# Attention and channel mix on one core: the weights' last bits on ScalarE, the last keys transposed as 64 columns, and a new early order

## The chip, the cores and the metric

The kernel runs on one core of one Trainium2 chip. The metric is the device time of one execution in microseconds (us); the kernel before takes 636.65 us as the median of three runs (635.62 to 637.12). The core has five engines with a queue each: TensorE (PE; its weight loads are listed as PEld), VectorE (DVE), ScalarE (ACT), GpSimd (POOL) and SyncE (SP), which here issues nearly all the DMAs.

## The reference, cut to what matters

There are 8 batches of 576 tokens, 8 heads of 64, a model width of 512 and a hidden width of 1024. Keys and values are averaged over groups of 8 tokens, so each batch has 72 of them. The attention's output is the input of a channel mix with a shift by one token.

```python
def _attn_ref(q, k, v):
    k_p = k.reshape(B, H, Sp, pool, D).mean(axis=3)
    v_p = v.reshape(B, H, Sp, pool, D).mean(axis=3)
    scores = scale * np.matmul(q, k_p.transpose(0, 1, 3, 2))
    scores = scores - np.max(scores, axis=-1, keepdims=True)
    attn = np.exp(scores)
    attn = attn / (np.sum(attn, axis=-1, keepdims=True) + 1e-09)
    return np.matmul(attn, v_p).astype(np.float32)

def _moe_ref(x, mu_k, mu_r, w_k, w_v, w_r):
    x_prev = np.concatenate([np.zeros((B, 1, D)), x[:, :-1, :]], axis=1)
    xk = mu_k * x + (1.0 - mu_k) * x_prev
    xr = mu_r * x + (1.0 - mu_r) * x_prev
    k = np.maximum(xk @ w_k, 0.0)
    v = k * k @ w_v
    r = 1.0 / (1.0 + np.exp(-(xr @ w_r)))
    return (r * v).astype(np.float32)
```

The three weight matrices are float64 in memory; everything else is float32.

## The kernel before, in words

**Tiles, chunks, precision.** The 4608 tokens are cut into 36 tiles of 128 rows and 12 chunks of 3 tiles (384 tokens). Matrix products of full precision are done in one of two ways. In chunk 0 the operands are float32 as they are ("whole"), which costs PE two passes for each product. From chunk 1 on each operand is split into a rounded high part and a low part (type fp32r), and a product is three: high by high, low by high, high by low.

**Weights.** They arrive as 20 blocks of 128 x 512 float64 words: wk0 to wk7 for the hidden layer, wr0 to wr3 for the gate, wv0 to wv7 for the output. `convert` (L415) turns the two 32-bit words of each number into a float32 by integer arithmetic, in five steps: ACT takes the absolute value of the top word (L427); DVE takes the maximum with a tiny number (L429), shifts left by 3 and masks (L431), merges sign and exponent (L436), and merges the low word's last three bits (L441). Later `split` (L450) makes a block's high part on ACT (L463) and its low part on DVE or POOL (L466, chosen by `LOW_BY`). There is one block of memory more than there are weight blocks, so the splits go one after another.

**Attention.** `keys`, `values` and `last_values` sum the eight tokens of each group: on DVE or POOL by halving (L473), or on PE as products with the identity (L484, "t" in `SUM_BY`). `softmax` (L572) does one tile: scores on PE (L592), then maximum, subtraction, exponential, sum and division, on DVE and ACT; for the tiles in `BY_HEAD` ACT does the eight heads one by one with the sum included (L614). The division is on POOL or DVE (`NORM_BY`). The 72 columns of a head are handled as 64 plus 8 ("last keys"), since PE takes 128 rows at a time: the 64 of two heads fill one transpose. `transposed` (L656) transposes the 64-column parts, four transposes a tile (L667). `transposed_rest` (L686) does the last keys: DVE copies the 8 columns of the eight heads twice in rounded form and once as the rest (L698, L700), so that there are 2 x 96 columns; PE transposes them in two products (L706) and ACT copies the 96 x 256 result out at once (L713). `attended` (L717) is the product with the values; for each pair of heads it needs the main part and the last keys of all three tiles of the chunk. `shifted` (L756) mixes in the previous token and `x_parts` (L793) splits the result.

**Channel mix.** For each chunk, `hidden` has 8 groups (L825), `gate` one per tile (L874), `mixed` one per tile (L906). In chunk 0 a group of `hidden` is 8 records in the trace, 4 products of two passes. The gate starts with the block wr0 and comes after the whole of `hidden`; the mixing comes after the gate, and so do the next chunk's attention products, since the operands' buffers are shared.

**What sets the order.** All work is written as generators that yield steps (engine, estimated length) and needs. The class `Order` (L71) runs them when the program is built, with a model of the engines, and emits the instructions in the order in which the model starts them; among steps that can start at about the same time the smallest due time goes first. `EARLIER` moves a few due times by hand. The result is one fixed order for each engine's queue. The loads follow the list `LOADS` on SP's queue, then go on tile by tile; q tiles have three slots, and the stage for keys and values three, plus four that lie in buffers which chunk 1 needs. `FILL` adds eight products of no use behind tile 1's scores. `SQUARED_ON_ACT` says how many groups of chunk 0's hidden layer are squared on ACT.

Of the kernel before, what the change touches and what calls it, by code (L numbers as in the profile page):

```python
# [10 lines left out]
I32 = mybir.dt.int32  # L11
AF = mybir.ActivationFunctionType
# [4 lines left out]
P = 128  # L17
# [12 lines left out]
WBUFS = 2 * NJT + NCT + 1  # L30

CHUNKS = [384] * 12
CH = max(CHUNKS)

WHOLE = (0,)
# [8 lines left out]
SUM_BY = {  # L44
    "k0": "t", "k1": "v", "v0": "t", "v1": "t", "r0": "t", "k2": "v", "k3": "v", "v2": "g", "v3": "g",
    "r1": "g",
}
# [10 lines left out]
COPIES_ON_ACT = 0  # L58

EARLIER = {  # L60
# [9 lines left out]

class Order:  # L71

    LATENCY = {"pe": 0.195, "dve": 0.13, "act": 0.14, "pool": 0.1, "sp": 0.0}

    def __init__(self):  # L80
        self.free = dict.fromkeys(self.LATENCY, 0.7)
        self.port = dict.fromkeys(self.LATENCY, 0.0)
        self.landed = 0.0
        self.now = 0.0
        self.made = {}
        self.slots = {}
        self.threads = []
        self.table = "exp"

    def add(self, due, steps, spare=0.0):  # L90

        given = [str(v) for v in steps.gi_frame.f_locals.values() if isinstance(v, (int, str))]
        due += EARLIER.get(" ".join([steps.gi_code.co_name, *given]), 0.0)
        self.threads.append([due, 0.0, None, steps, ("", 0.0), spare])

    def make(self, what, at=None):
        self.made[what] = self.now if at is None else at

    def give(self, kind, slot):
        self.slots.setdefault(kind, []).append((self.now, slot))  # L100

# [5 lines left out]
    @staticmethod  # L107
    def wait(t, until):
        t[1], t[4] = max(t[1], until), (t[4][0], max(t[4][1], until))

    def settle(self, t):

        while t[2] is None or t[2][0] in ("need", "take"):
            if t[2] is None:
                reply = None
            elif t[2][0] == "need":
                if any(w not in self.made for w in t[2][1:]):
                    return True
                self.wait(t, max(self.made[w] for w in t[2][1:]))
                reply = None  # L120
            else:
                have = self.slots.get(t[2][1])
                if not have:
                    return True
                at, reply = min(have, key=lambda h: h[0])
                have.remove((at, reply))
                self.wait(t, at)
            self.now = t[1]
            try:
                t[2] = t[3].send(reply)  # L130
            except StopIteration:
                return False
        return True

    def run(self):
        while True:
            self.threads = [t for t in sorted(self.threads, key=lambda t: t[0]) if self.settle(t)]
            ready = []
            for t in self.threads:
                if t[2][0] in ("need", "take"):  # L140
                    continue
                eng, _, lock = t[2][:3]
                at = max(
                    self.free[eng],
                    t[4][1] if t[4][0] == eng else t[1] + (t[5] if eng == "pe" else 0.0),
                )
                if lock:
                    at = max(at, self.port["pool" if eng == "dve" else "dve"])
                ready.append((at, t))
            if not ready:  # L150
                assert not self.threads, [t[2] for t in self.threads]
                return
            first = min(at for at, _ in ready)
            eng = next(t for at, t in ready if at == first)[2][0]
            at, t = min(
                ((at, t) for at, t in ready if t[2][0] == eng and at <= first + 0.1),
                key=lambda c: c[1][0],
            )
            _, length, lock = t[2][:3]
            func = t[2][3] if len(t[2]) > 3 else None  # L160
            if func and func != self.table:
                length, self.table = length + 1.3, func
            self.free[eng] = at + length
            if lock:
                self.port[eng] = at + length

            t[4] = (eng if eng == "pe" else "", at + length)
            t[1] = self.now = at + length + self.LATENCY[eng]
            try:
                t[2] = t[3].send(None)  # L170
            except StopIteration:
                self.threads.remove(t)


def dve(n, lock=True):
    return "dve", 0.05 + n / 960, lock
# [10 lines left out]
def pe(n, whole=False, times=1):  # L187
    return "pe", times * (2 * max(0.111, n / 1200 + 0.003) if whole else max(0.111, n / 2400 + 0.0155)), False
# [3 lines left out]
def attention_then_channel_mix(  # L192
# [41 lines left out]
    vbd_w = sb.tile([P, NPAIR, P], F32, name="vbd_w", tag="xkl")  # L234
# [9 lines left out]

    def operand(kind, c):
        if (kind, c) not in operands:
            dtype = F32 if c in WHOLE and kind != "ptr" else F32R
# [3 lines left out]
    slots("rs", CH // P, [P, DM])  # L251
# [5 lines left out]
    slots("px", 2, [P, 2, 4, KR])  # L257
    slots("pr", 2, [P, 2, 3, 4, KR], F32R)
    slots("mx", 2, [P, 2, 4, 1])
    slots("sm", 2, [P, 2, 4, 1])  # L260
    slots("vq", 1, [REM, 2, D], F32R)
    slots("tmp", 2, [P, WP])
# [33 lines left out]
    units = [stretches(a, n) for a, n in zip(starts, CHUNKS)]  # L296
    tiles = [
# [32 lines left out]
    def warm():  # L330
# [5 lines left out]
        for _ in range(WARMING):  # L336
            yield "pe", 0.86, False
# [4 lines left out]
    def fill(after, times):  # L342

        yield need(*after, "ident")
# [32 lines left out]
    def load(kind, i):  # L377
# [15 lines left out]
        if kind[0] == "w":  # L393
            yield "sp", 0.6, False
            got = sb.tile([P, 2 * WP], I32, name=f"got_{kind}{i}", tag="w", bufs=WBUFS)
            held["got", kind[1], i] = got
            nc.sync.dma_start(  # L397
# [17 lines left out]
    def convert(kind, i):  # L415
# [7 lines left out]
        low_word, top = w[:, :, 0], w[:, :, 1]  # L423
        ff = yield take("tmp")
        t = ff.bitcast(I32)
        yield act(WP)
        nc.scalar.activation(out=ff, in_=top.bitcast(F32), func=AF.Abs)  # L427
        yield "dve", 0.335, True
        nc.vector.tensor_scalar(out=ff, in0=ff, scalar1=TINY, scalar2=None, op0=ALU.max)  # L429
        yield "dve", 0.335, True  # L430
        nc.vector.tensor_scalar(  # L431
            out=t, in0=t, scalar1=3, scalar2=0x3FFFFFF8,
            op0=ALU.logical_shift_left, op1=ALU.bitwise_and,
        )
        yield dve(WP)
        nc.vector.scalar_tensor_tensor(  # L436
# [573 lines left out]
```

## Time and profile before

| | |
|---|---|
| median of three runs | 636.65 us (635.62 to 637.12) |
| the profiled execution | 637.05 us |
| its span, from the first to the last instruction | 635.3 us |
| PE busy | 621.9 us (98%) |
| DVE busy | 413.9 us (65%) |
| ACT busy | 334.4 us (53%) |
| POOL busy | 215.8 us (34%) |
| first attention product of chunk 0 | 25.31 us after the start |
| first hidden product of chunk 1 | 95.20 us |
| first hidden product of chunk 11 | 590.22 us |

The profile gives times from the first instruction of the execution. A row of the timeline has the start, the length, the engine, the line, the operation with output and inputs, and the number of instructions that it merges; PE's products are pipelined, and the length of a row holds the tail of its last product, under which the next row already runs, so the distance between starts tells what a product costs. A row of the waits has who waited for whom, the sum in us, how many times, and the longest. A row of the groups has the count, the sum and the mean of one in ns, and the idle time ahead of it.

### The profile page before, as it was taken

The page shows a single profiled execution, that of the slowest core. Times are in us where ns is not written, and L with a number is a line of the kernel's source. Part 1 is how long each engine was busy: PE and PEld are TensorE (multiplying, and loading weights), DVE is VectorE, ACT ScalarE, POOL GpSimd, SP SyncE. Part 2 cuts the span into 40 slices and gives each one's busy share as a digit, 9 for nine tenths or more (in the row PEclk, how much of TensorE's full clock was granted, in tenths as well). Part 3 has the DMA queues.
Part 4 walks back from the last instruction along what each step waited for, and adds up shares of the span by engine and source line. Part 5 has one row for each costly group of instructions (what it writes and reads, how often), then busy time and mean ns, then how long its engine had stood idle before and what let it go on. Part 6 is the DMA issues. An engine that isn't in the chain of part 4 may idle for free.

```text
span 635.3 us, 9068 instructions
## 1 busy us (share of the span) xinstructions
PE 621.9 (98%) x3256; PEld 538.6 (85%) x3256; DVE 413.9 (65%) x830; ACT 334.4 (53%) x688; POOL 215.8 (34%) x331
## 2 busy tenths in 40 slices
PE   7899999999999999999999999999999999999997
PEld 6754468889989989989988988988988988988986
DVE  5999998856979537647845665855854654653421
ACT  4667656855665644645454555546555455444420
POOL 1240348464435128028115018316405105203100
PEclk9999999999999999999999999999999999999999
DMA  9991130043314111033011061033110100000001
GB/s 293 364 390 62 33 125 35 15 126 142 91 51 172 61 35 51 0 142 108 17 35 51 0 202 49 16 109 125 33 34 34 35 17 34 18 0 35 18 0 50
DMA packets 35132, 50.91 MB, mean 80 GB/s; under 512 B 6544, under 2 KB 23184, under 8 KB 35088
## 3 DMA queue, kind: packets, MB, share of 16 engines
q1 hardware_dynamic: 34944, 50.22, 23.5%
q8 instruction: 25, 0.41, 0.3%
q14 instruction: 19, 0.16, 0.1%
q10 hardware_dynamic: 144, 0.13, 0.1%
HBM read 40.90 MB, written 9.44 MB: 79 GB/s over the span
## 4 chain that ended last, share of the span: by engine, by line
PE 84%; DMA 6%; DVE 5%; POOL 2%; SPq 1%; issue 1%; ACT 0%; DVEq 0%; POOLq 0%; ACTq 0%
PE mm L906 28%; PE mm L825 28%; PE mm L874 15%; PE bank L749 5%; PE sc L592 4%; DMA qs<-in_qT 4%; PE bank L667 2%; DMA got_wv<-in_w_v 1%; DMA got_wr<-in_w_r 1%; PE bank L706 1%; DVE tmp L436 1%; SPq L397 1%; POOL xkl L799 0%; DVE tmp L429 0%; POOL w_r L466 0%
## 5 line engine op out<-in xcount | busy, mean ns | idle before, releaser
L825 PE MATMUL mm<-xkh,w_k 128*128 128x384 f32 x704 | 182.2, 339 | 0.3 <-ACT xkh L797 0.3
L906 PE MATMUL mm<-w_v,sh 128*128 128x512 f32 x528 | 170.8, 392 | 0.0
L825 PEld LDWEIGHTS mm<-xkh,w_k 128*128 128x128 f32 x704 | 125.6, 188 | 1.5 <-issue 0.6
L825 PE MATMUL mm<-xkl,w_k 128*128 128x384 f32 x352 | 118.1, 336 | 0.7 <-POOL xkl L799 0.7
L906 PEld LDWEIGHTS mm<-w_v,sh 128*128 128x128 f32 x528 | 99.2, 188 | 19.8 <-issue 0.2
L906 PE MATMUL mm<-w_v,sl 128*128 128x512 f32 x264 | 103.0, 390 | 0.0
L642 POOL TENSOR_TENSOR px<-e,sm 128x64 f32<-128x64 f32 x32 | 11.4, 356 | 225.3 <-DVE sm L636 225.2
L874 PE MATMUL mm<-w_r,xrh 128*128 128x512 f32 x264 | 84.9, 394 | 0.0
L762 ACT ACTIVATE t<-bank,om_sb 128x384 f32<-128x384 f32 x96 | 48.8, 582 | 56.2 <-PE bank L749 56.1
L848 ACT CAST sh<-rk 128x384 fp32r<-128x384 f32 x88 | 45.2, 514 | 58.2 <-DVE rk L842 58.1
L781 DVE SCALAR_TENSOR_TENSOR xm<-bank,mu_sb,t 128x384 f32<-128x384 f32 x88 | 51.4, 612 | 35.2 <-POOL t L774 18.3
L850 DVE TENSOR_TENSOR sl<-rk,sh 128x384 fp32r<-128x384 f32 x88 | 53.5, 611 | 25.6 <-ACT sh L848 25.6
L825 PEld LDWEIGHTS mm<-xkl,w_k 128*128 128x128 f32 x352 | 66.1, 188 | 1.3 <-POOL xkl L799 1.3
L920 DVE TENSOR_TENSOR rs<-mm,rs 128x512 f32<-128x512 f32 (+1 forms) x37 | 24.8, 673 | 61.4 <-PE mm L906 61.4
L842 DVE SCALAR_TENSOR_TENSOR rk<-mm,rk 128x384 f32<-128x384 f32 x88 | 48.5, 553 | 16.4 <-ACT rk L835 15.8
L874 PEld LDWEIGHTS mm<-w_r,xrh 128*128 128x128 f32 x264 | 49.6, 188 | 10.0
L799 POOL TENSOR_TENSOR xkl<-xm,xkh 128x384 fp32r<-128x384 f32 x44 | 44.8, 1021 | 37.0 <-ACT xkh L797 36.6
L906 PEld LDWEIGHTS mm<-w_v,sl 128*128 128x128 f32 x264 | 49.7, 188 | 9.0
L473 POOL TENSOR_TENSOR stage<-stage 128x512 f32<-128x512 f32 (+5 forms) x60 | 51.0, 857 | 14.1 <-DMA stage<-in_vm 6.6
L835 ACT ACTIVATE rk<-mm 128x384 f32<-128x384 f32 x88 | 42.9, 488 | 23.3 <-PE mm L825 22.7
L874 PE MATMUL mm<-w_r,xrl 128*128 128x512 f32 x132 | 51.4, 389 | 0.0
L605 DVE TENSOR_REDUCE mx<-sc 128x8 f32<-128x576 f32 x35 | 26.3, 752 | 31.4 <-PE sc L592 31.4
(117 smaller groups left out, 979.2 us busy)
## 6 DMA issues: line engine op xcount, KB each, us to landing
out<-rs SPq DMA_DIRECT2D x35, 256.0 KB, 2.0
stage<-in_kT SPq DMA_DIRECT2D x15, 576.0 KB, 5.0
qs<-in_qT SPq DMA_DIRECT2D x32, 256.0 KB, 3.2
stage<-in_vm SPq DMA_DIRECT2D x14, 512.0 KB, 6.5
got_wk<-in_w_k SPq DMA_DIRECT2D x8, 512.0 KB, 9.2
got_wv<-in_w_v SPq DMA_DIRECT2D x8, 512.0 KB, 10.0
stage<-in_vr SPq DMA_DIRECT2D x7, 384.0 KB, 4.1
got_wr<-in_w_r SPq DMA_DIRECT2D x4, 512.0 KB, 8.3
```

The costliest lines, as they stand in the source:

```text
L473: nc_eng.tensor_tensor(out=st[:, :, :w], in0=st[:, :, :w], in1=st[:, :, w:2 * w], op=ALU.add)
L749: nc.tensor.matmul(out=xp[:, o], lhsT=v, rhs=p, start=(q == 0), stop=(q == len(terms) - 1))
L762: nc.scalar.activation(out=t[:, m, 1:n + 1], in_=xp, func=AF.Copy, scale=om_sb[:, m, g:g + 1])
L781: nc.vector.scalar_tensor_tensor(out=xm[:, :n], in0=xp, scalar=mu_sb[:, m, g:g + 1], in1=t[:, m, :n], op0=ALU.mult, op1=ALU.add,)
L799: nc.gpsimd.tensor_tensor(out=lo, in0=xm[:, :n], in1=hi, op=ALU.subtract)
L825: nc.tensor.matmul(out=hp, lhsT=w[:, o], rhs=x[:, ct, :n], start=(ct == 0 and k == 0), stop=(ct == NCT - 1 and k == len(terms) - 1),)
L835: nc.scalar.activation(out=rk[:, :n], in_=hp, func=AF.Relu)
L842: nc.vector.scalar_tensor_tensor(out=rk[:, :n], in0=hp, scalar=0.0, in1=rk[:, :n], op0=ALU.max, op1=ALU.mult)
L848: nc.scalar.copy(out=sh[:, :n], in_=rk[:, :n])
L850: nc.vector.tensor_tensor(out=operand("sl", c)[:, jt, :n], in0=rk[:, :n], in1=sh[:, :n], op=ALU.subtract)
L874: nc.tensor.matmul(out=bank, lhsT=x[:, ct, o], rhs=w, start=(ct == 0 and k == 0), stop=(ct == NCT - 1 and k == len(terms) - 1),)
L906: nc.tensor.matmul(out=bank, lhsT=s[:, o], rhs=w, start=(jt == 0 and k == 0), stop=(jt == NJT - 1 and k == len(terms) - 1),)
```

## The change

There are five parts.

1. *Conversion.* ACT's absolute value is scaled by 2^-112, which puts the exponent where a float32 has it, so that the maximum (L429) and the merge of the sign and exponent (L436) fall away. The low word's last three bits are put beside the top word's sign by a copy of 16-bit words, on ACT for 16 blocks and as a shift on DVE for 4 (`LAST_BITS_BY`). DVE keeps one shift and one merge.
2. *Last keys.* PE transposes the 8 columns of the eight heads as they are, 64 columns, once per tile; the split comes behind it, out of PSUM: two ACT copies of 32 rows, two DVE subtractions, two more ACT copies. In chunks 0 and 1 this is done tile by tile, from chunk 2 on for three tiles at once (`REST_BY`), in one PSUM bank. There are four buffers for the untransposed columns instead of two.
3. *Loads.* The list has another order, in which k1 comes first, the blocks of wk come out of order, wk3 is the last of them and wr0 the last load of all.
4. *Who does what.* k0 and v0 are summed on DVE (before: PE), k2 on PE (before: DVE); tile 1's softmax goes by head and tile 2's no longer does, tiles 5 and 6 do; tile 1's division is on POOL; more low parts are made on DVE; seven groups are squared on ACT instead of eight; the eight filling products are gone.
5. *Order.* The model of the engines has other lengths, knows a slow PE clock in the first 60 us, and takes due times for some 150 steps from a table (`DUE`). A weight block's memory is handed out as a slot, so the splits may come in another order. `PARTS` has one entry, so chunk 0 is still done in one part, and all four of its stages are still whole. The zeroed values of chunk 0 (`vbd_w`) lie in another buffer.

The diff, cut to its core:

```diff
-WBUFS = 2 * NJT + NCT + 1
+WSLOTS = 2 * NJT + NCT + 1
...
-TINY = 2.0**-15
+DOWN = 2.0**-112
...
 LOADS = (
-    "k0 k1 q0 q1 wk0 v0 v1 wk1 c0 q2 r0 wk2 wk3 k3 wk4 v3 v2 q3 wk5 r1 k2 wk6 wk7 q4 wr0 q5 wr1 wr2 "
-    "wr3 wv0 wv1 wv2 wv3 wv4 wv5 wv6 wv7 "
+    "k1 k0 q0 wk1 q1 v0 q2 wk5 v1 c0 v2 k3 wk0 r0 wr3 k2 wk2 wk7 q5 q3 wk6 v3 wv7 q4 wk4 wk3 "
+    "wv6 wv3 wr1 r1 wv1 wv4 wv2 wv0 wr2 wv5 wr0 "
 )
...
-NORM_BY = {0: "v", 1: "v", 2: "v", 3: "v"}
+NORM_BY = {0: "v", 1: "g", 2: "v", 3: "v", 7: "v", 5: "g", 4: "g", 8: "g", 6: "g"}
...
-FILL = (([("scored", 1)], 8),)
+FILLS = ((("scored", 1), 0),)
+LAST_BITS_BY = {"k": "aaaaavaa", "r": "aava", "v": "aaaavaav"}
-LOW_BY = {"k": "gvgvgvgv", "r": "gvgv", "v": "gvgggvgv"}
-BY_HEAD = (0, 2)
+LOW_BY = {"k": "vgvgvvvv", "r": "vvgv", "v": "gvvvggvg"}
+BY_HEAD = (0, 1, 5, 6)
-SQUARED_ON_ACT = 8
+SQUARED_ON_ACT = 7
+REST_BY = (1, 1, 3)
...
+    slots("px", 4, [P, 2, 4, KR])
...
+        quarters = got.bitcast(U16).rearrange("p (n four) -> p n four", four=4)
...
-        nc.scalar.activation(out=ff, in_=top.bitcast(F32), func=AF.Abs)
-        nc.vector.tensor_scalar(out=ff, in0=ff, scalar1=TINY, scalar2=None, op0=ALU.max)
+        nc.scalar.activation(out=ff, in_=top.bitcast(F32), func=AF.Abs, scale=DOWN)
+        if LAST_BITS_BY[kind][i] == "a":
+            nc.scalar.activation(
+                out=quarters[:, :, 2], in_=quarters[:, :, 1], func=AF.Copy, scale=2.0**-13, bias=2.0**-14 - 0.5
+            )
+        else:
+            nc.vector.tensor_scalar(
+                out=quarters[:, :, 2], in0=quarters[:, :, 1], scalar1=13, scalar2=None,
+                op0=ALU.logical_shift_right,
+            )
-        nc.vector.tensor_scalar(
-            out=t, in0=t, scalar1=3, scalar2=0x3FFFFFF8,
-            op0=ALU.logical_shift_left, op1=ALU.bitwise_and,
-        )
-        nc.vector.scalar_tensor_tensor(
-            out=t, in0=top, scalar=-0x40000000, in1=t, op0=ALU.bitwise_and, op1=ALU.bitwise_or
-        )
+        nc.vector.tensor_scalar(out=t, in0=t, scalar1=3, scalar2=None, op0=ALU.logical_shift_left)
         nc.vector.scalar_tensor_tensor(
-            out=got[:, :WP], in0=low_word, scalar=29, in1=t,
-            op0=ALU.logical_shift_right, op1=ALU.bitwise_or,
+            out=got[:, :WP], in0=top, scalar=-0x7FFFFFF9, in1=t, op0=ALU.bitwise_and, op1=ALU.bitwise_or
         )
...
-    def transposed_rest(i):
-        for k in (0, 2):
-            nc.vector.tensor_copy(out=pr[:, :, k], in_=px)
-        nc.vector.tensor_tensor(out=pr[:, :, 1], in0=px, in1=pr[:, :, 0], op=ALU.subtract)
-        for r in range(2):
-            nc.tensor.transpose(
-                out=rp[:REM, r, :],
-                in_=pr[:, r].bitcast(F32).rearrange("p c h k -> p (c h k)"),
-                identity=ident,
-            )
-        nc.scalar.copy(out=operand("ptr", c)[:, :, o], in_=rp[:REM, :2, :])
+    def transposed_rest(c, first, n):
+        yield need(*[("px", first + j) for j in range(n)], *([("attended", c - 1)] if c else []))
+        for j in range(n):
+            nc.tensor.transpose(
+                out=bank[:8 * KR, j * P:(j + 1) * P], in_=px.rearrange("p a h k -> p (a h k)"), identity=ident
+            )
+        rp, ptr = bank[:, :n * P], operand("ptr", c)
+        rows = 4 * KR
+        for r in range(2):
+            nc.scalar.copy(out=ptr[:rows, r, o], in_=rp[r * rows:(r + 1) * rows])
+        for r in range(2):
+            nc.vector.tensor_tensor(
+                out=ptr[rows:2 * rows, r, o], in0=rp[r * rows:(r + 1) * rows], in1=ptr[:rows, r, o],
+                op=ALU.subtract,
+            )
+        for r in range(2):
+            nc.scalar.copy(out=ptr[2 * rows:, r, o], in_=rp[r * rows:(r + 1) * rows])
```

More of the change, by code (lines that the diff above doesn't have):

```diff
@@ L11 @@
 I32 = mybir.dt.int32
+U16 = mybir.dt.uint16
 AF = mybir.ActivationFunctionType
@@ L105, in fetched, with advance @@
         self.make(what, self.landed)
[L107 to L128, printed above, removed]
+    def advance(self, t):
+        while True:
+            reply = None
+            if t.step is not None:
+                if t.step[0] == "need":
+                    for w in t.step[1:]:
+                        if w not in self.made:
+                            self.waiting.setdefault(w, []).append(t)
+                            return
+                    until = max([self.made[w] for w in t.step[1:]])
+                else:
+                    have = self.slots.get(t.step[1])
+                    if not have:
+                        self.takers.setdefault(t.step[1], []).append(t)
+                        return
+                    until, reply = got = min(have, key=lambda h: h[0])
+                    have.remove(got)
+                t.at = max(t.at, until)
+                if t.pe_at is not None:
+                    t.pe_at = max(t.pe_at, until)
+            self.now = t.at
@@ L129, in settle @@
             try:
-                t[2] = t[3].send(reply)
+                t.step = t.steps.send(reply)
             except StopIteration:
-                return False
-        return True
-    def run(self):
[L136 to L145, printed above, removed]
-                )
[L147 to L157, printed above, removed]
-            )
[L159 to L162, printed above, removed]
@@ new lines, in advance, with stretch @@
+                return
+            if t.step[0] not in ("need", "take"):
+                self.ready.append(t)
+                return
+    def stretch(self, at, length):
+        if at > 60:
+            return length
+        self.bursts = [b for b in self.bursts if b[1] > at - self.WINDOW]
+        busy = sum(b[1] - max(b[0], at - self.WINDOW) for b in self.bursts) / self.WINDOW
+        if busy < 0.39:
+            self.slow = True
+        elif busy > 0.93:
+            self.slow = False
+        length *= 1 + self.slow
+        self.bursts.append((at, at + length))
+        return length
@@ L261, in attention_then_channel_mix @@
     slots("vq", 1, [REM, 2, D], F32R)
+    for i in range(WSLOTS):
+        order.give("w", i)
     slots("tmp", 2, [P, WP])
@@ L340, in warm, with fill @@
         order.give("tmp", zeros)
-    def fill(after, times):
-        yield need(*after, "ident")
+    def fill(what, times):
+        yield need(what, "ident")
         bank = yield take("bank")
@@ L468, in split @@
         )
+        order.give("w", held.pop(("slot", kind, i)))
         order.make(("parts", kind, i))
@@ L523, in values @@
             r = slice(h2 * D, (h2 + 1) * D)
[L524 to L526 removed]
+            nc.scalar.copy(out=(vbd_w if as_is else vbd_h[i])[r, gs, r], in_=o[r])
+        if not as_is:
+            yield "dve", 0.6, True
             for h2 in range(2):
@@ L541, in values @@
             )
-            order.make(("value parts", b, p))
-        else:
-            order.make(("value parts", b, p))
+            held["spent", p] = True
+            if ("spent", 1 - p) in held:
+                order.give("rs", for_rs[0])
+        order.make(("value parts", b, p))
     def last_values(b):
@@ L714, in transposed_rest, with attended @@
         order.give("bank", bank)
-        order.make(("side", i))
-    def attended(c, g):
-        n = CHUNKS[c]
-        whole = c in WHOLE
-        mine = [i for i, t in enumerate(tiles) if t[0] == c]
+        for j in range(n):
+            order.make(("side", first + j))
+    def attended(c, g, p):
+        off, n = parts[c][p]
+        segs = stretches(starts[c] + off, n)
+        as_is = whole(c, "p")
+        mine = [i for i, t in enumerate(tiles) if t[0] == c and off <= t[1] < off + n]
@@ L928, in attention_then_channel_mix @@
     order.add(-10, constants())
-    for after, times in FILL:
-        order.add(-25, fill(after, times))
+    for what, times in FILLS:
+        order.add(-25, fill(what, times))
     order.add(4, complements())
```

308 lines of the change are left out of this document (173 added, 135 removed), and 49 rows, old and new, of tables (DUE, EARLIER).

## The prediction

> **What bounds the kernel now.** I read the page's head first, then the busy time of each engine in stretches that I cut at the kernel's own stages, then PE's waits inside the early stretches, and last the order of time on PE, VectorE (DVE) and ScalarE (ACT). The columns of the stretches are the length, the busy time of PE, weight loads, DVE, ACT and GpSimd (POOL) with instruction counts, the granted clock and the DMA share.
>
> ```profile
> span 635.3 us, 9068 instructions
> ```
> ```profile
> 25.30:55.00 29.70, 27.69 (x89) 16.31 (x90) 29.09 (x62) 20.04 (x44) 11.38 (x18) 1.00 0.88 312
> 55.00:95.20 40.20, 38.37 (x150) 20.25 (x149) 39.13 (x78) 23.94 (x43) 12.90 (x18) 1.00 0.18 63
> 95.20:105.00 9.80, 8.87 (x50) 7.63 (x49) 7.84 (x15) 5.80 (x12) 9.50 (x16) 1.00 0.14 54
> 105.00:590.20 485.20, 485.20 (x2640) 439.18 (x2638) 308.73 (x609) 260.94 (x519) 179.06 (x273) 1.00 0.19 60
> ```
>
> There are two regimes. From 105 to 590 us PE is busy for 485.20 of 485.20 us at full clock, so there an instruction less on PE is time gained and work taken from any other engine is worth nothing. From 25.3 us (the first attention product) to 95.2 us (the first product of chunk 1's hidden layer) DVE is busy for 29.09 of 29.70 and 39.13 of 40.20 us. It looks like the bound, but PE is nearly full as well. What DVE costs there is what PE waits for:
>
> ```profile
> PE mm L825 <- DVE xkh L781: 2.0, 2, 1.0
> PE mm L874 <- DVE got_wr L441: 1.3, 1, 1.3
> PE mm L825 <- POOL xkl L799: 0.7, 2, 0.5
> PE bank L706 <- DVE pr L700: 0.4, 1, 0.4
> PE mm L825 <- ACT xkh L797: 0.3, 1, 0.3
> PE mm L906 <- DVE got_wv L441: 0.2, 1, 0.2
> ```
>
> The four rows that name DVE come to 3.9 us and lie before 95.2; the other two, 1.0 us, lie between 95.2 and 105. So a DVE with nothing to do could give at most about 4.9 us from 25.3 on, however many microseconds of DVE work go.
>
> **The change part by part.**
>
> *DVE steps of the weights' conversion.* Two blocks are converted here in turn, four DVE steps each:
>
> ```profile
> 49.12 0.75 DVE L429 TENSOR_SCALAR tmp<-tmp 128x512 f32<-128x512 f32 x2
> 49.79 0.75 DVE L431 TENSOR_SCALAR tmp<-tmp 128x512 int32<-128x512 int32 x2
> 50.46 1.28 DVE L436 SCALAR_TENSOR_TENSOR tmp<-got_wr,tmp 128x512 int32<-128x512 int32 x2
> 51.66 1.28 DVE L441 SCALAR_TENSOR_TENSOR got_wr<-got_wr,tmp 128x512 int32<-128x512 int32 x2
> 52.86 0.22 DVE L642 TENSOR_TENSOR px<-e,sm 128x64 f32<-128x64 f32 x1
> ```
>
> From start to start that is 3.74 us for two blocks, 1.87 each. The change keeps one shift (0.67/2 = 0.34) and one merge (1.20/2 = 0.60): 0.94 each, so 20 blocks give back 18.6 us of DVE. Four blocks take the last bits out on DVE; no row shows a 16-bit shift, and between 0.34 (L431) and 0.60 (L441) I take 0.5, so 2 us come back and 16.6 stay away. The other DVE edits (k0 and v0 summed there rather than on PE, k2 the other way, tile 1's softmax by head on ACT and its division on POOL, two more of wk's low parts) I estimate to cancel to within 2 us. DVE's 68 us in the two stretches fall to about 52 of 70, and it no longer limits there.
>
> *ACT takes the last bits of 16 blocks.* Nothing before copies 16-bit words on ACT. The nearest row is a block's absolute value:
>
> ```profile
> 47.31 1.27 ACT L427 ACTIVATE tmp<-got_wr 128x512 f32<-128x512 f32 x2 [0.86 <-DVE got_wk L441]
> 48.56 0.63 ACT L509 COPY kbd<-early_ptl 64x144 f32<-64x144 f32 x2
> ```
>
> That is 0.62 from start to start; I take 0.62, with 0.3 (as a DVE shift) and 1.25 (half rate) as ends: 10 us in all (5 to 20), spread over 10 to 85 us. The second ACT step lies beside DVE's shift, so a block's own chain goes from 0.62 + 0.34 + 0.34 + 0.60 + 0.60 = 2.5 to 0.62 + 0.62 + 0.60 = 1.8 us; that counts only where PE waits for a block, which is in the 3.9 already.
>
> *The last keys.* Each 128-row tile has its transposes on PE; L667 is the main part, L706 the last keys':
>
> ```profile
> 64.78 0.60 PE L667 MATMUL bank<-ident,pm 128*128 128x128 f32 x4
> 65.21 0.38 PE L706 MATMUL bank<-ident,pr 128*96 128x128 f32 x2
> 65.43 1.88 PE L906 MATMUL mm<-got_wv,sh 128*128 128x512 f32 x4
> ```
>
> Two of L706 hold PE for 0.22 us, 0.11 each (0.38 includes the tail, under which the next one runs). One is left per tile, so 36 go. Those of tiles 0 to 2 lie before 25.3, where PE has gaps; the other 33 lie where it is full or nearly so: 33 x 0.11 = **3.6 us**. What replaces them on ACT and DVE is priced from
>
> ```profile
> L713 ACT CAST ptr<-bank 96x256 fp32r<-96x256 f32 x36 | 13.3, 370 | 0.2 <-PE bank L706 0.2
> L842 DVE SCALAR_TENSOR_TENSOR rk<-mm,rk 128x384 f32<-128x384 f32 x88 | 48.5, 553 | 16.4 <-ACT rk L835 15.8
> ```
>
> From chunk 2 on, three tiles together need four ACT copies of 384 columns and two DVE subtractions of 384: 4 x 0.45 + 2 x 0.55 = 2.9 us, against 3 x 0.37 on ACT plus three casts and subtractions on DVE. ACT and DVE are 54% and 64% busy from 105 to 590, so the 0.7 us more on ACT per chunk costs nothing by itself. As a chain it runs from the transposes to the attention product, which waits for it, with the whole PE queue behind. For chunk 6, during chunk 5's mixing, the room is this:
>
> ```profile
> 324.24 0.38 PE L706 MATMUL bank<-ident,pr 128*96 128x128 f32 x2
> 329.94 0.34 PE L749 MATMUL bank<-pth,vbd_h 128*128 128x384 f32 x1
> ```
>
> From 324.46 (two transposes at 0.11) that is 5.5 us of room, against 2.9 of work, some 0.5 for five hand-overs and whatever is ahead in ACT's queue. I take nothing for it; the cover is the mixing products that PE runs meanwhile, and a late chain would cost its lateness once a chunk (rival below). One of three PSUM banks is held for these 3.4 us, while attention products take turns on the others.
>
> *First loads anew.* Loads go out on SP's one queue and land in order at the rate of the whole, so I read landing times by the bytes ahead. k3 was the load with 5952 KB up to and with it; r0 now has the same 5952 KB, having had 4352.
>
> ```profile
> 12.24 0.33 SPq L411 DMA_DIRECT2D early_ptl<-in_kT  x1
> ```
> ```profile
> early_ptl<-in_kT SPq DMA_DIRECT2D x1, 576.0 KB, 8.2
> ```
>
> r0 thus lands at 12.24 + 8.2 = 20.4. Behind it come PE's sum and the steps to the first use:
>
> ```profile
> 5.03 2.17 PE L484 MATMUL mm<-stage,ident 128*128 128x144 f32 x16
> 23.95 0.26 ACT L553 CAST vq<-mm 96x128 fp32r<-96x128 f32 x1
> 25.76 0.63 PE L749 MATMUL bank<-ptr,vbd_r 96*128 96x384 f32 x1
> ```
>
> About 1.9 for the sum and 1.8 from L553 to L749 make 24.1, so the first attention product, at 25.3 now, can start at most **1.2 us** earlier: q2, three places further up, no longer sets it, r0 does. k2's sum moves from DVE to PE, and k2 lands after r0: **2.0 us** more on PE (16 products, as L484). The last load is now wr0, which the gate needs first, behind every hidden product on PE. Loads fill 0.88 of 25.3 to 55, so it lands by 51.4 and is converted by 53.5 or so. wk3, needed fourth, has 11392 KB up to it:
>
> ```profile
> 31.38 7.54 DMA got_wr<-in_w_r
> ```
> ```profile
> 37.99 15.10 PE L825 MATMUL mm<-xkh,got_wk 128*128 128x384 f32 x46 [1.02 <-DVE xkh L781]
> ```
>
> wr1 had 11776 KB and landed at 38.9, so wk3 lands near 37.9 and is ready by 40.5. The last five hidden products take 5 x 8 x 0.325 = 13.0 us and end at 53.5, just as wr0 is ready. So chunk 0 keeps its gate near 53, as now, and PE has room before that for chunk 1's scores, transposes and k2's sum. q5 and q3 take slots of q that tiles 0 and 1 gave back long before; no other load waits behind a slot.
>
> *Sum*, against the profiled execution's 637.05 us (1.75 more than its span): 3.6 for the transposes; 1.2 from the earlier start; of the 3.9 us of PE's waits 2.9 go, because k2's sum and scores fill the holes, and 1.0 stays for wk3 and wr0; minus 2.0 for k2's sum; 0.7 of the 1.0 us of waits after 95.2. Together 6.4: 630.65. The median of the runs is 0.4 under the profiled one, so I forecast **630.3 us**.
>
> **The rivals.**
>
> *ACT becomes the bound of the early stretch.* Between 25.3 and 55 ACT has 20.04 of 29.7 us. Add eight or so last-bit copies (5), the four copies of the last keys for tiles 2 to 4 (2), tiles 4 and 5's softmax brought forward (an estimated 4): 31. Against it: the later wv blocks and the splits of wk can wait until after 55, where 16 us are free. If it holds, the waits do not go and some 1.5 are added: only 3.6 + 1.2 - 2.0 - 1.5 remain, 635.3 as a median. The Trainium skill, page "ScalarE: Activation LUTs", section "Rules for kernel authors", advises VectorE rather than ScalarE for simple arithmetic; by it, this rival would be the outcome. The trace speaks for it only in that ACT is this full; DVE is fuller.
>
> *The clock.* The filling products after tile 1's score go, and v0's and k0's sums leave PE. PE had a slow spell before:
>
> ```profile
> 15.00:20.00 5.00, 4.79 (x27) 4.79 (x28) 4.12 (x16) 1.76 (x9) 0.00 (x0) 0.66 1.02 367
> ```
> ```profile
> 15.21 2.14 PE L592 MATMUL sc<-kbd,qs 128*128 128x144 f32 x8 [1.36 <-DMA qs<-in_qT]
> 27.05 1.22 PE L592 MATMUL sc<-kbd,qs 128*128 128x144 f32 x8
> ```
>
> A score took 2.14 there and 1.22 later; 0.66 over 5 us is 3.4 us at half rate, 1.7 us of work lost. If such a spell comes at 24 us, on the path, the forecast loses 1.7: 632.0. The Trainium skill, page "TensorE: Matmul & The Clock Gate", Part 1, says that a window of about 3.4 us with PE idle halves the clock until one such window is busy; that agrees with the 3.4 above and would put a spell where PE starves before r0. Against it: PE has v1's and r0's sums and three tiles between 10 and 24, which at half rate would keep it full.
>
> *Slower: the last keys come late in every chunk.* ACT's queue holds a table load (1.28) right where the copies for chunk 6 would stand:
>
> ```profile
> 325.31 1.28 ACT L628 ACT_TABLE_LOAD   x1
> ```
>
> With the table load and two or three steps of about half a microsecond ahead, the chain's 3.4 us become some 6, and the room is 5.5; PE then stands still for the difference, once in each of ten chunks. From 0.64 us late per chunk on it eats the gain; 1.0 late gives 630.3 + 10 = 640.3. Against it: the mixing products leave 8 us more before the hidden layer needs the results, so the products can stand later in PE's order.
>
> **How the numbers follow.** The forecast has 0.60, ACT as the bound 0.18, the slow clock 0.14, late last keys 0.08. The forecast's own range is 628 (all waits go) to 633 (none of the early ones). Taking in the clock rival and most of ACT's, and a us below for what the waits table does not list, gives 627 to 635 for 8 in 10. A measurement of this kernel can tell about 0.2%, 1.3 us, from no change, so faster means under 635.4: 0.86, with most of ACT's rival in it; same 0.05; slower 0.09.
>
> **What would show it.** Right: L429 and L436 gone, DVE at most 80% busy from 25 to 90; one transpose of the last keys per tile, PE still full after 105 us, and 3.2 us less from there to the end; the first attention product near 24; chunk 1's hidden layer starting at 92 to 93 instead of 95.2. Wrong: PE waiting on ACT's conversion or on wr0 around 53; gaps on PE ahead of L749's successor in every chunk; a granted clock under 1 after 24 us; a 16-bit copy of over 1 us on ACT.

## The result and the profile after

| | before | after |
|---|---|---|
| median (8 runs each) | 636.77 us (635.62 to 637.41) | 639.37 us (638.59 to 642.0) |
| profiled execution | 637.05 us, span 635.3 | 642.0 us, span 640.1 |
| first attention product | 25.31 | 28.36 |
| first hidden product of chunk 0 | 29.26 | 32.90 |
| first hidden product of chunk 1 | 95.20 | 100.22, without a break from 107.34 |

The changed kernel is slower: the ratio is 1.005, with an interval of 1.0032 to 1.0068. Forecast were 630.3 us and a gain. The profiled execution of after is the slowest of its eight runs, 2.6 us over their median, so small differences between the two traces are read with care below.

The stretches of after, cut at the same times as those of before (length, busy time of PE, weight loads, DVE, ACT and POOL, granted clock, DMA share, GB/s):

```profile
20.00:25.30 5.30, 5.30 (x34) 5.18 (x32) 3.54 (x10) 4.71 (x13) 1.06 (x2) 0.66 1.02 387
25.30:55.00 29.70, 25.48 (x105) 16.23 (x104) 27.05 (x56) 26.14 (x51) 8.09 (x16) 0.94 0.95 320
55.00:95.20 40.20, 37.12 (x128) 19.50 (x128) 27.74 (x52) 39.35 (x80) 7.99 (x11) 1.00 0.18 63
105.00:590.20 485.20, 483.57 (x2625) 437.58 (x2625) 290.58 (x544) 268.34 (x522) 177.43 (x268) 1.00 0.18 58
```

The third row carries the story. Before, DVE was busy for 39.13 of these 40.20 us and ACT for 23.94; now DVE has 27.74 and ACT 39.35. The work went off DVE as forecast, and ACT is now the full engine. From 105 us on PE is full again (the 1.63 us that it lacks are a single wait at 105.7, the third row of the waits below). PE's waits of after, from the first attention product on:

```profile
PE mm L905 <- ACT vq L631: 1.9, 1, 1.9
PE mm L905 <- DVE xkh L860: 1.7, 1, 1.7
PE mm L905 <- POOL xkl L878: 1.6, 1, 1.6
PE bank L774 <- POOL px L722: 1.1, 1, 1.1
PE mm L988 <- ACT rs L963: 0.9, 1, 0.9
PE mm L988 <- DVE got_wv L526: 0.7, 1, 0.7
PE mm L988 <- ACT w_r L539: 0.4, 1, 0.4
```

Together 8.3 us, where before had 4.9 and the forecast left 1.3. Three rows name ACT, and the chain behind the third row, which names POOL, also runs through ACT. From 91 us to the end of that wait at 107.34, the chain of work that ended last is this (start, length, engine, what):

```profile
90.98 0.51 ACT w_k L539
91.48 1.26 ACT got_wv L513
92.78 1.05 ACT t L840 x2
...
96.87 1.28 ACT L694
98.16 0.78 ACT e L694 x5
100.69 1.89 ACT t L840 x4
105.33 1.97 POOL xkl L878 x2
107.34 5.12 PE mm L905 x28
```

The second row is the new step: L513 takes the last bits out, 1.26 us by itself in a queue whose next entry, L840, takes up chunk 1's attention output, for which PE waits at the end. It is not alone: the softmax of another tile (L694) with its table load stands in the same queue from 96.87 to 100.69. Some groups of ACT up to 108 us give the price of the new step and that of the absolute value (L510):

```profile
L513 ACT ACTIVATE got_wk<-got_wk 128x512 uint16<-128x512 uint16 x7 | 9.5, 1355 | 0.1
...
L513 ACT ACTIVATE got_wv<-got_wv 128x512 uint16<-128x512 uint16 x6 | 8.1, 1346 | 0.0
...
L510 ACT ACTIVATE tmp<-got_wk 128x512 f32<-128x512 f32 x8 | 5.4, 680 | 0.6 <-DMA got_wk<-in_w_k 0.6
...
L513 ACT ACTIVATE got_wr<-got_wr 128x512 uint16<-128x512 uint16 x3 | 4.1, 1354 | 0.0
```

The 16-bit copy takes 1.35 us, twice the 0.68 of an activation with as many words. From start to start it can be less:

```profile
63.16 1.35 ACT L513 ACTIVATE got_wr<-got_wr 128x512 uint16<-128x512 uint16 x1
64.23 0.35 ACT L782 CAST ptr<-bank 32x128 fp32r<-32x128 f32 x1
```

That is 1.07 here, and up to 1.39 elsewhere in this run. Against the 0.62 that the forecast took, sixteen copies cost 7 to 12 us more of ACT.

PE's own saving came. From chunk 2's first hidden product to chunk 11's, before and after:

```profile
146.37 0.60 PE L825 MATMUL mm<-xkh,w_k 128*128 128x384 f32 x2
590.06 0.51 PE L825 MATMUL mm<-xkh,w_k 128*128 128x384 f32 x2
```
```profile
155.82 0.60 PE L905 MATMUL mm<-xkh,w_k 128*128 128x384 f32 x2
594.49 0.51 PE L905 MATMUL mm<-xkh,w_k 128*128 128x384 f32 x2
```

443.69 us became 438.67, 5.02 less. In this stretch after has 27 transposes and two scores fewer, the scores having been done earlier; a score is 8 products, about 1 us. So some 3 us are the transposes' (0.11 each), and 9.45 us had been lost before chunk 2 began.

### The profile page after: what moved, and what is told of

Read it like the earlier page. It is cut to its first block, busy times and chain, and to the rows that moved or that the text cites. A ratio compares the mean times of both kernels' runs of the same rounds, so it can differ in the third digit from the quotient of the medians.

```text
span 640.1 us, 8886 instructions
## 1 busy us (share of the span) xinstructions
PE 618.4 (97%) x3188; PEld 534.3 (83%) x3188; DVE 380.7 (59%) x723; ACT 371.8 (58%) x761; POOL 211.2 (33%) x327
## 4 chain that ended last, share of the span: by engine, by line
PE 83%; ACT 2%; POOL 0%; DVE 0%; issue 0%; DVEq 0%
PE mm L905 29%; PE mm L988 28%; PE mm L956 14%; PE bank L833 5%; PE sc L670 4%; PE bank L747 2%; ACT t L840 1%; PE bank L774 1%; ACT e L694 0%; POOL xkl L878 0%; ACT L694 0%; ACT got_wv L513 0%; ACT w_k L539 0%; ACT kbd L586 0%; POOL xrl L878 0%
## 5 line engine op out<-in xcount | busy, mean ns | idle before, releaser
L956 PE MATMUL mm<-w_r,xrh 128*128 128x512 f32 x264 | 86.2, 397 | 0.0
L840 ACT ACTIVATE t<-bank,om_sb 128x384 f32<-128x384 f32 x96 | 49.1, 583 | 55.9 <-PE bank L833 55.2
L550 POOL TENSOR_TENSOR stage<-stage 128x512 f32<-128x512 f32 (+8 forms) x60 | 52.5, 888 | 24.6 <-DMA stage<-in_kT 10.4
L670 PE MATMUL sc<-kbd,qs 128*128 128x144 f32 (+1 forms) x312 | 41.5, 292 | 5.9 <-ACT kbd L586 3.3
```

The lines of the kernel that those rows point to most:

```text
L550: nc_eng.tensor_tensor(out=st[:, :, :w], in0=st[:, :, :w], in1=st[:, :, w:2 * w], op=ALU.add)
L670: nc.tensor.matmul(out=halves[g // 2][o:o + n, 0, k:k + 2 * KEYS], lhsT=qs[:, g, o:o + n], rhs=kbd[b % 2][:, g, :], start=True, stop=True,)
L840: nc.scalar.activation(out=t[:, m, 1:n + 1], in_=xp, func=AF.Copy, scale=om_sb[:, m, g:g + 1])
L956: nc.tensor.matmul(out=bank, lhsT=x[:, ct, o], rhs=w, start=(ct == 0 and k == 0), stop=(ct == NCT - 1 and k == len(terms) - 1),)
```

## The experiments

The theory after the result was that the length of ACT's 16-bit copy eats the gain. The rivals: the slow clock at 15 to 25 us, the new last keys, and DVE being the bound all the same. The written-out order is made from estimated lengths, so "order kept" below means that each engine has the instructions of the named kernel in its order, apart from the ones edited; "planned anew" means that the model of the engines made another order. All ratios are against before, run beside them.

### Short copies

After, order kept. The copy covers 256 of 512 columns only, so half of the last bits are left as they are.

```diff
-                out=quarters[:, :, 2], in_=quarters[:, :, 1], func=AF.Copy, scale=2.0**-13, bias=2.0**-14 - 0.5
+                out=quarters[:, :WP // 2, 2], in_=quarters[:, :WP // 2, 1], func=AF.Copy, ...
```

> The changed kernel, each queue's order kept, but the 16 copies of last bits on ACT cover 256 of 512 columns (for the other half of the columns the last bits are left as the top word has them, so that part of the computation is left out). Theory ACT: the copy takes 1.35 us and holds ACT for 1.10, not 0.62, so ACT is full from 55 to 107 us and PE waits for it; at about 0.6 each ACT sheds some 8 us, chunk 1's hidden layer starts 5 to 7 us earlier, and the time is 632 to 635. Theory clock (PE at half rate from 16 to 25 us costs the start): nothing changes there, 638 to 640. Theory loads (r0, wk3 and wr0 come late): 638 to 640 as well.

Measured: 632.97 us (632.31 to 633.64), ratio 0.995 (0.9937 to 0.9962). The copies take 0.78 us and after's loss is gone: 6.4 us less than after.

```profile
55.00:95.20 40.20, 39.22 (x135) 20.91 (x134) 30.59 (x58) 38.82 (x98) 13.06 (x24) 1.00 0.28 93
```

ACT is still busy for 38.82 us, but it now does 98 instructions in this stretch and not 80, and PE has 39.22 us instead of 37.12. The copy's length is the main cause.

### A warm clock

After, order kept, with eight more warming products and twelve filling ones behind tile 1's scores.

```diff
+        for _ in range(8):
+            nc.tensor.matmul(out=bank[:, :256], lhsT=zeros[:, :P], rhs=zeros[:, :256], start=True, stop=True)
...
-        for _ in range(times):
-            yield pe(P, True)
+        for _ in range(12):
```

> The changed kernel with the order of everything else kept, plus 8 more warming products before the first scores and 12 filling products behind tile 1's scores, so that PE is not idle between 5 and 15 us. Theory clock: no half rate from 16 to 25 us, the first attention product comes 2 to 3 us earlier and the time is 636 to 637.5. Theory ACT: the first product may come earlier, but ACT is behind from 55 us on whatever the start, so under 1 us is won: 638.5 to 640.

Measured: 638.89 us (638.53 to 640.82), ratio 1.0051 (1.0038 to 1.0064), as after. The slow spell between 20 and 25 us went in part, the one behind it wholly, and little came of it:

```profile
20.00:25.30 5.30, 4.61 (x35) 4.34 (x34) 3.54 (x10) 5.13 (x14) 1.29 (x2) 0.85 1.01 367
25.30:55.00 29.70, 25.52 (x111) 16.52 (x112) 26.87 (x56) 27.75 (x56) 8.29 (x16) 1.00 0.96 325
```

The clock is 0.85 and 1.00 against 0.66 and 0.94, yet PE's busy time from 25.3 to 55 is the same 25.5 us, and the first attention product came at 28.14 instead of 28.36. Two other runs agree: one of after's eight was granted a clock of 0.998 over the whole and still took 638.59 us, and one of the half copies was granted 0.99 and took 632.97. The clock is not the cause.

### The two parts alone, planned anew

Before, with only the new last keys, and before, with only the new conversion; the order was planned anew for each.

> The kernel before with only the new way for the last keys (one transpose of 64 columns a tile, split behind it, three tiles at once from chunk 2 on, four buffers). The step of the prediction: 33 transposes at 0.11 us on a full PE, so 3.6 us less, 633. The rival that the last keys come late in every chunk: 637 or more.

> The kernel before with only the new conversion (16 copies of last bits on ACT, 4 shifts on DVE, two DVE steps a block), its own loads and due times. Theory ACT: 16 copies at 1.10 take ACT from 49 of 75 us to 67 between 20 and 95, some of them ahead of what PE waits for; DVE's relief and ACT's delay meet, 636 to 640. If DVE's relief alone counted: its 3.9 us of waits go, 633.

Measured: 645.87 us, ratio 1.0161 (1.0143 to 1.0179), and 647.99 us, ratio 1.0186 (1.0172 to 1.02). Both are slower than before and after; the first lies in its rival's range (637 or more), the second beyond both of its ranges. In the first PE waits for 4.8 us at one place (L823 for L779's result), in the second for 4.1 us at another (L672 for L703's). These runs change a part and the whole order at once, so they cannot price the parts, and the parts were tried again with the order kept (below).

### The last bits shifted on DVE

After, order kept; the sixteen copies become 16-bit shifts on DVE.

```diff
-            nc.scalar.activation(
-                out=quarters[:, :, 2], in_=quarters[:, :, 1], func=AF.Copy, scale=2.0**-13, bias=2.0**-14 - 0.5
+            nc.vector.tensor_scalar(
+                out=quarters[:, :, 2], in0=quarters[:, :, 1], scalar1=13, scalar2=None,
+                op0=ALU.logical_shift_right,
```

> The changed kernel, each queue's order kept, but the 16 copies of last bits leave ACT and stand as shifts at the same places on DVE. Theory ACT: ACT sheds 16 x 1.10 = 17.6 us, DVE takes 16 x 0.52 = 8.3 and stays under 90% from 55 to 95; PE's waits on ACT go, 630 to 633, no slower than with half copies (632.97). Rival, DVE is the bound again: 635 to 638.

Measured: 636.95 us (635.5 to 642.04), ratio 1.0014 (0.9998 to 1.0031). That is 2.4 us less than after, and no gain on before.

```profile
25.30:55.00 29.70, 25.26 (x101) 15.48 (x100) 28.45 (x58) 18.29 (x42) 9.22 (x16) 0.94 0.95 321
```

ACT has room here (18.29), and DVE is nearly full again (28.45 of 29.70). PE's waits that name DVE are 3.9 us from the first attention product on, against 2.4 in after, and the shifts take 0.74 to 0.87 us instead of the 0.52 expected. The rival's range of 635 to 638 held. That DVE binds once more is likely but not shown by its busy time: in the kernel with whole words below, DVE has 28.62 us in this stretch, and the kernel is 2.4 us faster.

### The last keys transposed twice

After, order kept, with each last-keys transpose issued twice (36 more products that change nothing).

> The changed kernel, order kept, each transpose of the last keys given out twice: 36 more on PE, as many as the change took away. If one costs 0.11 us on a full PE, 30 of them count (those of tiles 0 to 5 stand where PE waits for ACT): 639.4 + 3.3 = 642.7. If they hide, 639.4.

Measured: 642.79 us (641.29 to 645.3), ratio 1.0106 (1.0085 to 1.0126): 3.4 us over after, or 0.095 each. This holds the forecast's term, 0.11 us for each transpose on a full PE.

### The copy's true length in the plan

After, with the copy's estimated length raised in the plan, and planned anew.

```diff
-            yield "act", 0.57, False
+            yield "act", 1.15, False
```

> The changed kernel with one number of its model altered: the copy on ACT is planned as 1.15 us, not 0.57, so the order is made anew with the same due times. If the order was bad only because of the wrong length, this recovers most of it, 633 to 636. If ACT simply has too much to do, the order helps little, 638 to 641. Since due times were not made for it, the result can also be worse by several us.

Measured: 661.47 us (660.84 to 662.69), ratio 1.0394 (1.0379 to 1.0409). The order made with a truer number is 22 us worse; between 25.3 and 55 us PE is busy for only 16.67 us, at a granted clock of 0.68. The due times in the table were made for the other length, as the expectation feared.

### The forms of the copy

Six kinds of activation, four of each, put behind the end of after's work on ACT, so that they wait for nothing.

> The changed kernel with 24 ACT copies of 512 columns behind its last step, four each of: 16-bit words with a step of four to the same (as the change has it); 16-bit contiguous to contiguous; 16-bit step four to float32; float32 to 16-bit step four; float32 step two to float32; 16-bit contiguous to float32. If the step of the 16-bit words is what costs, the first takes 1.35 us and the contiguous one 0.68; if the 16-bit type does, all forms with 16-bit output or input take 1.35; if the 16-bit write does, the first, second and fourth.

This single run took 661.11 us, with the added work at its end. In order, the forms are: 16 bits with a step of 8 bytes to the same; 16 bits without a step to the same; 16 bits with a step of 8 bytes to float32; float32 to 16 bits with a step of 8 bytes; float32 with a step of 8 bytes to float32; 16 bits without a step to float32. The groups of the first four, one row for each (behind the bar the sum in us and the mean in ns):

```profile
L1072 ACT ACTIVATE stage<-stage 128x512 uint16<-128x512 uint16 x4 | 5.3, 1334 | 19.4 <-DVE stage L1061 19.3
```
```profile
L1072 ACT ACTIVATE stage<-stage 128x512 uint16<-128x512 uint16 x4 | 2.5, 629 | 0.1
```
```profile
L1072 ACT ACTIVATE stage<-stage 128x512 f32<-128x512 uint16 x4 | 2.6, 661 | 0.1
```
```profile
L1072 ACT ACTIVATE stage<-stage 128x512 uint16<-128x512 f32 x4 | 5.3, 1336 | 0.1
```

1334 and 1336 ns belong to the two forms that write 16-bit words 8 bytes apart, whatever they read. Reading with the same step costs some 30 ns (661, and 660 for the fifth form), and the 16-bit type itself costs nothing (629, and 629 for the sixth form). The Trainium skill, page "ScalarE: Activation LUTs", section "What ACT_TABLE_LOAD costs", gives 186 ns and 0.833 ns for each element, for float32 and bfloat16 alike; by it 512 elements are an estimated 612 ns. That is near the 629 to 661 here and not near the strided 16-bit write.

### The last bits as whole words

After, order kept. ACT writes the last bits as an int32 over the low word instead of as 16 bits beside the sign, and DVE's shift takes them in.

```diff
-                out=quarters[:, :, 2], in_=quarters[:, :, 1], func=AF.Copy, scale=2.0**-13, bias=2.0**-14 - 0.5
+                out=low_word, in_=quarters[:, :, 1], func=AF.Copy, scale=2.0**-13, bias=2.0**-14 - 0.5
...
-        nc.vector.tensor_scalar(out=t, in0=t, scalar1=3, scalar2=None, op0=ALU.logical_shift_left)
+        nc.vector.scalar_tensor_tensor(
+            out=t, in0=t, scalar=3, in1=low_word, op0=ALU.logical_shift_left, op1=ALU.bitwise_or
+        )
...
```

> The changed kernel, order kept, but ACT writes the last bits as 32-bit words over the low word, and DVE takes them in with its shift (a two-input step of 0.60 instead of 0.34); the result is the same bits. By the copy forms a 16-bit input with 32-bit output takes 0.65 us instead of 1.35, so ACT sheds what half copies shed (632.97), and DVE gets 20 x 0.26 = 5 us more. Theory ACT: 633 to 635, faster than both kernels. If DVE's 5 us count fully where DVE is at 90% (25 to 55 us), 636.

Measured: 634.57 us (633.96 to 635.89), ratio 0.9966 (0.9953 to 0.9978). This one does the whole computation and is faster than both kernels: 1.9 us less than before, 4.8 less than after. ACT's copy and DVE's step, which has grown:

```profile
L513 ACT ACTIVATE got_wk<-got_wk 128x512 int32<-128x512 uint16 x7 | 4.7, 677 | 0.1
```
```profile
L523 DVE SCALAR_TENSOR_TENSOR tmp<-tmp,got_wk 128x512 int32<-128x512 int32 x8 | 5.4, 688 | 2.7 <-ACT got_wk L513 2.7
```

The copy is back at 0.68 us. DVE pays for it with 0.69 on wk and 0.76 over all 20 blocks, instead of the 0.48 that the shift takes in after (mean of 20), and is busy for 31.21 us from 55 to 95.2 instead of 27.74. Its earlier stretch is nearly full:

```profile
25.30:55.00 29.70, 26.14 (x114) 16.90 (x113) 28.62 (x57) 24.20 (x55) 8.66 (x16) 1.00 0.93 316
```

### The parts alone, with the order of before kept

Three kernels: before with the new last keys, taken tile by tile in all chunks; before with the new conversion and its 16-bit copies; before with both, the last bits as whole words.

> The kernel before with each queue's order kept and only the last keys done the new way, tile by tile in all chunks: one transpose where two stood, and the split (four ACT copies, two DVE subtractions) where one ACT copy stood. If the 645.87 of the last keys alone came from the order made anew, not from the part: 36 transposes less, 3.6 us, minus up to 1 for subtractions that wait on ACT in DVE's queue: 632.5 to 634. If the part itself is late: 637 or more.

> The kernel before with each queue's order kept and only the new conversion: the 16 copies of 16-bit words stand right behind the absolute values on ACT. Theory ACT with before's order: ACT goes from 44 of 70 us between 25 and 95 to some 58, not full, but each block is ready 1.1 later while DVE is 0.94 sooner: 634 to 638, so the conversion's own gain is small, and the 647.99 came from the order made anew. If DVE's relief counts fully: 633.

> The kernel before with each queue's order kept, the last keys as in the run with only them, and the conversion with the last bits as 32-bit words. If the two parts' gains add: 3 from the transposes and 1 to 3 of the 4.9 us of waits that DVE caused, 630 to 633, the fastest so far. If waits only change places: 633 to 634.

Measured: 639.23 us (638.4 to 639.93), ratio 1.0041 (1.0028 to 1.0054); 643.14 us (641.5 to 643.67), ratio 1.0098 (1.0083 to 1.0113); 637.31 us (636.32 to 639.01), ratio 1.001 (1.0 to 1.002). All three came out worse than expected.

For the last keys the trace shows where the time went. From chunk 2's hidden layer to chunk 11's it takes 440.71 us, against before's 443.69: 2.98 us less, which is 27 transposes at 0.11. But chunk 2's hidden layer begins at 150.68 instead of 146.37. Of these 4.31 us, 1.88 are lost by the first attention product, which comes at 27.19 instead of 25.31. Ahead of it PE waits for ACT, and from 25.3 to 55 us its granted clock is 0.90, where before's was 1.00:

```profile
PE bank L667 <- ACT vbd_w L524: 2.9, 1, 2.9
```
```profile
25.30:55.00 29.70, 27.95 (x88) 16.90 (x89) 28.16 (x61) 20.13 (x47) 11.14 (x18) 0.90 0.88 309
```

One tile's last keys on ACT, in before and in this kernel:

```profile
18.73 0.37 ACT L713 CAST ptr<-bank 96x256 fp32r<-96x256 f32 x1
18.99 0.33 ACT L614 ACTIVATE e<-sc,mx 128x72 f32<-128x72 f32 x1
```
```profile
17.66 0.52 ACT L704 CAST ptr<-bank 32x128 fp32r<-32x128 f32 x2
18.95 0.52 ACT L711 CAST ptr<-bank 32x128 fp32r<-32x128 f32 x2 [0.77 <-DVE ptr L706]
19.50 0.32 ACT L614 ACTIVATE e<-sc,mx 128x72 f32<-128x72 f32 x1
```

Before: 0.26 us until ACT's next step. New: 1.84, because ACT copies twice, stands still for 0.77 until DVE has subtracted, and copies twice again, while the by-head exponentials of the next tile (L614) wait in its queue. Two tiles of this lie ahead of the first attention product; the third stands on ACT from 27.03 on, ahead of the first product that reads the last keys (28.50, before 25.76).

For the conversion, sixteen copies of 1.35 us again (mean 1351 on wk), and PE's two longest waits are the start of the attention, where before waited for 0.6 us, and chunk 0's mixing, where it waited for 0.2:

```profile
PE bank L753 <- DVE got_wk L446: 3.2, 1, 3.2
PE mm L910 <- ACT w_k L467: 3.1, 1, 3.1
```

The first attention product comes at 27.76. With both parts and the cheap copies it comes at 28.00, and yet the time is only 0.8 us over before, which is hardly clear of noise. So on before's order the parts gain nothing; it is with after's loads, order and shares of work that the cheap copy gives 1.9 us.

## Why the prediction was wrong, point by point

**The step that failed first: "I take 0.62".** The copy was priced by the absolute value's row, with half rate as the far end. The far end was the truth: 1.35 us long, 1.07 to 1.39 from start to start. ACT then had 39.35 of 40.20 us from 55 to 95.2, and the first rival, ACT as the bound, came true. It was priced at 635.3, with 1.5 us added to the 4.9 of waits; they grew to 8.3. Its counterargument, that 16 us of ACT are free after 55, failed on the same number. Halving the copies alone takes back 6.4 of the 9.1 us by which the forecast was missed. With cheaper copies the kernel lies at 632.97 (half copies) and 634.57 (words), inside the range of 627 to 635.

**The step that failed second: "the first attention product ... can start at most 1.2 us earlier".** It was built on r0: landing at 20.4, 1.9 us for its sum, 1.8 from there to the product. With half copies PE waited for r0 until 21.62, and from L631, which takes up its sum at 23.64, to the product it took 3.5 us, not 1.8:

```profile
21.62 1.99 PE L561 MATMUL mm<-early_xrl,ident 96*96 96x128 f32 x16 [0.32 <-DMA early_xrl<-in_vr]
...
25.21 2.13 PE L561 MATMUL mm<-stage,ident 128*128 128x144 f32 x16
27.18 0.81 PE L833 MATMUL bank<-pth,rs 128*128 128x384 f32 x2
27.53 0.63 PE L833 MATMUL bank<-ptr,vbd_r 96*128 96x384 f32 x1
```
```profile
26.79 0.90 ACT L791 CAST ptr<-bank 32x128 fp32r<-32x128 f32 x4
```

Two things end there at nearly the same time. The second row is k2's sum, which fills PE right up to the first attention product. The last row is the last step of the last keys of tiles 1 and 2, and the first product that reads them starts at 27.53. In the sum, ACT's steps for the last keys were costed only from chunk 2 on, and there at nothing; that they can delay the start by themselves is shown by the run with the new last keys as the only edit (27.19). What k2's sum costs beside them is not shown, since no run took it away. With the last bits off ACT altogether the product still came at 26.63. Together the two terms were to lose 0.8 us, and they lost 1.9 in the run with half copies.

**A third step: "chunk 0 keeps its gate near 53".** The gate's first product came at 62.71 in after and at 57.81 with half copies, against 52.93 before, each time right behind other work on PE. How much of this is only work done earlier was not separated.

**The waits: "2.9 go".** Even with half copies 3.9 of 4.9 us stayed. PE's waits there, all after 27 us:

```profile
PE mm L905 <- DVE xkh L860: 1.2, 1, 1.2
PE mm L905 <- POOL xkl L878: 1.1, 1, 1.1
PE mm L988 <- DVE got_wv L526: 1.0, 2, 0.5
PE mm L905 <- ACT sh L917: 0.6, 1, 0.6
```

Three of the four rows name DVE or POOL, as before, though DVE now has 30.59 of 40.20 us from 55 to 95.2. So relieving DVE did not remove these waits. Whether what is left belongs to the chain of attention, mixing and split itself or to ACT, which has 38.82 of these 40.20 us, is not shown.

The account against before's span of 635.3 us, in us gained:

| term | forecast | half copies | after |
|---|---|---|---|
| transposes | 3.6 | 3.6 | 3.6 |
| start of the attention, k2's sum | 1.2 - 2.0 = -0.8 | 25.31 - 27.18 = -1.9 | 25.31 - 28.36 = -3.05 |
| PE's waits from there on | 2.9 + 0.7 = 3.6 | 4.9 - 3.9 = 1.0 | 4.9 - 8.3 = -3.4 |
| sum | 6.4 | 2.7 | -2.85 |
| measured on the span | | 635.3 - 631.7 = 3.6 | 635.3 - 640.1 = -4.8 |

The transposes' term is taken as forecast in all three columns. 0.9 us of the half copies' gain is not accounted for. Of the 1.95 that after's profile is worse than its sum, most can be the slow clock between 25.3 and 55 us (0.94 of 29.7 is 1.8 us of work lost), which this execution had and the one with more filling products had not; no run shows it by itself. After's median is 2.6 us under its profiled run.

**Right:** the transposes at 0.11 us each (2.98 us for 27 with before's scores, 3.4 for 36 added ones); PE as the only bound after 105 us; L429 and L436 gone and DVE at 78% from 25 to 90, where at most 80% was forecast (it is 91% from 25.3 to 55 and 69% from 55 to 95.2). The hidden layer of chunk 1 at 92 to 93 came only with half copies (92.41).

**The other rivals.** The clock had its spell where it was feared (0.66 from 20 to 25.3), but curing it in part, and the one behind it wholly, moved next to nothing. The last keys did not come late in every chunk: PE is full from 107.34 on. They came late in chunk 0 instead. The advice of the Trainium skill that stood beside the first rival (page "ScalarE: Activation LUTs", section "Rules for kernel authors": VectorE rather than ScalarE for simple arithmetic) gave the right outcome for this kernel: with the last bits on DVE it is 2.4 us faster than after. But the copy in words on ACT is another 2.4 faster (636.95 against 634.57), so it was the form of the write that decided, not the engine.

**Open.** Whether chunk 0's last keys done in the old way, with everything else as in the kernel with words, would give back some of what is lost at the start was not tried, nor was k2's sum left on DVE.

## What to carry to other kernels

Price an operation by a row with the same type and the same step on the written side; when no row has it, let the far end of the price decide whether the plan stands, because an engine with 16 us to spare takes 16 copies of 0.62 us and not 16 copies of 1.07 to 1.39. A chain that costs nothing in the steady state still has to be priced at the start, where the first product waits for it and its engine's queue has no slack. In a kernel with a written-out order, compare parts with the order kept: made anew, the order left the two parts 5 to 7 us worse than with the order kept (645.87 against 639.23, where the last keys also went three tiles at a time, and 647.99 against 643.14), and one corrected length made it 22 us worse.

## What the hardware showed that was not expected

On ACT the write of 16-bit words 8 bytes apart takes 1334 to 1355 ns for 512 columns, 629 to 661 when the words are written without a step, and 677 as 32-bit words 8 bytes apart; the step on the read side costs some 30 ns. On DVE the 16-bit shift with the same step took 742 to 940 ns in the changed kernel, while the 32-bit shift that took its place in the kernel with words took 419 to 421. The rows of wk, one block each:

```profile
L518 DVE TENSOR_SCALAR got_wk<-got_wk 128x512 uint16<-128x512 uint16 x1 | 0.7, 742 | 0.0
```
```profile
L518 DVE TENSOR_SCALAR got_wk<-got_wk 128x512 int32<-128x512 int32 x1 | 0.4, 421 | 0.0
```

A transpose is listed with 272 ns, but on a full PE one more costs 0.095 to 0.11 us.
